# Attention and a mixture of experts on one core: the upper half of the hidden columns computed in transposed form

## The chip, the cores and the metric

The kernel runs on one core of a Trainium2 chip. The metric is device time in microseconds, the median of the timed runs. TensorE multiplies: the stationary operand is loaded as weights, the moving operand streams past it column by column, and results are summed in PSUM. ScalarE and VectorE work element by element, GpSimd issues the gathers and scatters, SyncE issues the other DMAs, in the order of its queue.

## The reference

Attention with a sigmoid in place of the softmax, then a mixture of eight experts, each token going to the one with the largest logit:

```python
B, heads, S, D = 8, 12, 448, 64          # 3584 tokens of width 768
attn = 1 / (1 + exp(-(q @ k.T / 8 - log(S))))
x = (attn @ v)                            # laid out as [3584, 768]
logits = normed(x) @ normed(expert_emb).T / tau
e = argmax(logits); gate_w = softmax(logits)[e]
for e in range(8):                        # w1 [768, 1024], w2 [1024, 768]
    h = maximum(x[mask] @ w1[e], 0)
    out[mask] = gate_w[mask] * (h @ w2[e])
```

## The kernel before

Attention comes first (to about 355 us of the span): 48 pairs of heads, scores, sigmoid and the product with v, with the routing worked out beside it. Then the expert stage. The tokens of an expert are cut into tiles of 128; a last piece of at most 64 tokens is a short tile. Two early tiles (numbers -2 and -1) of the expert with the most tokens are computed while the routing still runs, then tiles 0, 1, 2 and so on, 33 slots, of which 31 hold tokens here. Even slots take experts from the front and odd slots from the back, and each parity has its own buffers for w1 and w2, so that a new expert's weights are loaded for one parity while the other computes.

All values are split in two halves of 16 bits, hi and lo, and a product is three terms: hi x hi, hi x lo, lo x hi (`L1_TERMS`, `L2_TERMS`).

A tile t goes through these steps. GpSimd gathers its token rows (`xg`), SyncE transposes them by DMA to `xt`. Layer 1 has `xt` blocks stationary and w1 moving, 18 matmuls of 512 columns for each half of the 1024 hidden columns (`layer1_full`, L213); in a short tile the two halves run side by side in the two column halves of the array (`layer1_short`, L219). The result has tokens on partitions, in PSUM tile `pss`, one for each half. `hidden` then takes the ReLU, hi by ScalarE (L239), lo by VectorE (L240), to `hr`, and SyncE transposes `hr` by DMA to `hT` (L242), with hidden columns on partitions, as layer 2 needs it. Both halves do so, one after the other. Layer 2 has `hT` blocks stationary and w2 moving, 48 matmuls of 384 columns (L225, short: L232), lower half of the hidden columns first. The result is scaled and scattered to `out` (L780, L781, L912).

The order is written by hand. TensorE does layer 1 of tile t+1, then layer 2 of tile t. For the other engines a string, `ORD = "aGbLcdCDAMB"`, says the order of one step: small letters fetch weight blocks (a, d: halves of w2; b, c: halves of w1), capitals cast them, G gathers and transposes `xt` of tile t+3, L is layer 1 of t+1 with its ReLU and its transposes, M is layer 2 of t. SyncE's queue therefore holds, over one step and into the next: the transposes of `hT`, then c, d, a, then the transpose of `xt`, then b, and the next transposes of `hT`. Fetches and casts are skipped where the expert stays the same. Short or full is chosen at run time by a branch of TensorE (`tc.If(kind > 0)`), and both kinds are written out in its program.

Of the kernel before, what the change touches and what calls it, by code (L numbers as in the profile page):

```python
# [11 lines left out]
F16 = mybir.dt.float16  # L12
# [9 lines left out]
P = 128  # L22
# [11 lines left out]
NFC = F // P  # L34
# [15 lines left out]
ORD = "aGbLcdCDAMB"  # L50
ED = 2
# [58 lines left out]
def attn_moe_kernel(ctx: ExitStack, tc: tile.TileContext, q, k, v, emb, tau, w1, w2, consts, eye, out, dbg=None):  # L110
# [98 lines left out]
    L2_TERMS = [(fc, i, wi) for fc in range(NFC) for i, wi in ((0, 2), (0, 3), (1, 2))]  # L209

    def layer1_full(t, st, xt, half):
        for n, (kc, wi, xi) in enumerate(L1_TERMS):
            nc.tensor.matmul(ph[half][:, t % 2], xt[:, xi, kc, :], wts[st][wi][:, kc, half * HF:(half + 1) * HF],  # L213
                             start=(n == 0), stop=(n == len(L1_TERMS) - 1))

    def layer1_short(t, st, xt):
        for n, (kc, wi, xi) in enumerate(L1_TERMS):
            for s in range(2):
                nc.tensor.matmul(ph[0][s * HP:(s + 1) * HP, t % 2], xt[:, xi, kc, :HP], wts[st][wi][:, kc, s * HF:(s + 1) * HF],  # L219
                                 start=(n == 0), stop=(n == len(L1_TERMS) - 1))  # L220

# [6 lines left out]
    def layer2_short(st, hs, po):  # L228
        for n, (fc, i, wi) in enumerate(L2_TERMS):
            for d in range(2):  # L230
                s = fc // 4 * HP
                nc.tensor.matmul(po[0][d * HP:(d + 1) * HP, :HD], hs[0][:, i, fc % 4, s:s + HP],  # L232
                                 wts[st][wi][:, fc, d * HD:(d + 1) * HD],
                                 start=(n == 0), stop=(n == len(L2_TERMS) - 1))

    def hidden(t, half):
        ps = ph[half][:, t % 2]
        hr = bp2.tile([P, 2, HF], F16, name=f"hr{half}", bufs=1)
        mark[ET.Activation] = nc.scalar.activation(hr[:, 0], ps, AF.Relu)  # L239
        mark[ET.DVE] = nc.vector.scalar_tensor_tensor(hr[:, 1], ps, 0.0, hr[:, 0], op0=ALU.max, op1=ALU.subtract)  # L240
        h = bp2.tile([P, 2, HF // P, P], F16, name=f"hT{half}")
        mark[ET.SP] = nc.sync.dma_start_transpose(h.rearrange("f i c t -> f (i c) t"), hr.rearrange("t i f -> t (i f)"))  # L242
        hT[t, half] = h
# [12 lines left out]
    with ExitStack() as actx:  # L256
# [388 lines left out]
        layer1_full(-2, 0, xte[0], 0)  # L645
        hidden(-2, 0)
# [7 lines left out]
        layer1_full(-2, 0, xte[0], 1)  # L654
        hidden(-2, 1)
# [6 lines left out]
        layer1_full(-1, 0, xte[1], 0)  # L662
        psn = route2(NG - 1)
        hidden(-1, 0)
# [132 lines left out]
    layer1_full(-1, 0, xte[1], 1)  # L797
    hidden(-1, 1)
# [96 lines left out]
    def layer1(t, st, xt):  # L895
        kind = short(t)
        with pe_guard(t):
            with tc.If(kind > 0) as br:
                layer1_short(t, st, xt)
            with br.Else():  # L900
                for half in range(2):
                    layer1_full(t, st, xt, half)
        for half in range(2):
            hidden(t, half)
# [46 lines left out]
    for t in range(MAXL):  # L951
# [6 lines left out]
        if t == 0:  # L958
            layer1(1, 1, xg_t.pop(1))
            for n in range(2):  # L960
                reload(2, 0, n)
            place(wb[1][1:])
            for n in range(2):
                reload(1, 1, n)
            reload(3, 0, 1, fetch=True)
            reload(2, 1, 0, fetch=True)
            layer2(0, 0)
            reload(3, 0, 0)
            continue
        parts = {"a": (t + 1, 1, 1), "b": (t + 3, 0, 0), "c": (t + 3, 0, 1), "d": (t + 2, 1, 0)}  # L970
        casts = {"A": parts["a"], "B": parts["b"], "C": (t + 2, 0, 1), "D": (t + 1, 1, 0)}
# [38 lines left out]
```

## Time and profile before

| | |
|---|---|
| timed runs, median (lowest to highest of 3) | 887.71 us (884.38 to 889.79) |
| the profiled execution, whole time | 880.52 us |
| its span, first to last instruction | 878.7 us |
| mean granted clock of TensorE | 0.979 |
| TensorE busy | 825.4 us, 94% of the span |
| VectorE, ScalarE busy | 400.7 and 402.7 us, 46% each |
| DMA queue of SyncE | 63.9% of 16 engines' span |

Busy time of TensorE is the union of its matmuls; the mean length of one matmul is longer than the distance between two, since they are pipelined. Times in the rows below are counted from the start of the span. In a row of the timeline the first number is the start, the second the length of the stretch, xN the count of instructions, and in brackets the idle time just before it and what ended it. SPq stands for SyncE's queue.

### The profile page before, as it was taken

Reading aid. Unit: us, or ns where it says so; the run is one execution under the profiler, and the core shown is the slowest. Engines: PE = TensorE matmul, PEld = TensorE weight load, DVE = VectorE, ACT = ScalarE, POOL = GpSimd, SP = SyncE. Lnnn points to the kernel's source line nnn. Section 1 sums busy time; section 2 is a strip of 40 time slices with the busy share of each in tenths; the row PEclk is TensorE's granted clock in tenths of the full one; section 3 lists DMA queues with packets and bytes.
Section 4 is the critical chain, followed back from the end, with each engine's and each line's share of the span. In section 5 each row is a group of like instructions: output and inputs, shape, how many; then the busy total and the mean of one; then the engine's idle time right before and its main releaser. Section 6 shows DMA issues by size and latency. Waiting matters only on the chain. (4 is left out here: it accounts for less than half of the span.)

```text
span 878.7 us, 16153 instructions
## 1 busy us (share of the span) xinstructions
PE 825.4 (94%) x5384; PEld 402.3 (46%) x5384; DVE 400.7 (46%) x765; ACT 402.7 (46%) x616; POOL 180.4 (21%) x238
## 2 busy tenths in 40 slices
PE   6999999999999999998699999699999999999784
PEld 3444444444444443454345555355555555555342
DVE  4434354446576865776244116543510113515642
ACT  5667677767676766133133015433410113314541
POOL 2112121212121220123212212112222122223010
PEclk9999999999999999999989999899999999999897
DMA  5646475658797985969899579999996568879984
GB/s 148 165 112 195 122 194 148 174 136 201 209 243 198 266 200 170 199 144 240 196 274 183 127 191 301 252 223 246 261 163 136 104 134 234 236 195 273 283 210 85
DMA packets 260113, 170.67 MB, mean 194 GB/s; under 512 B 199804, under 2 KB 237158, under 8 KB 259984
## 3 DMA queue, kind: packets, MB, share of 16 engines
q1 hardware_dynamic: 249632, 132.96, 63.9%
q0 software_dynamic: 9360, 35.81, 13.1%
q8 instruction: 67, 1.10, 0.5%
q14 instruction: 62, 0.51, 0.2%
q10 hardware_dynamic: 992, 0.29, 0.1%
HBM read 103.80 MB, written 23.99 MB: 145 GB/s over the span
## 5 line engine op out<-in xcount | busy, mean ns | idle before, releaser
L213 PE MATMUL pss<-w,xt 128*128 128x512 f16 x900 | 198.5, 379 | 1.8 <-DVE hr L240 0.9
L225 PEld LDWEIGHTS <-hT 128*128 128x128 f16 x1296 | 129.2, 100 | 121.2 <-DMA hT<-hr 28.5
L355 ACT ACTIVATE att<-pss,bias_s 128x896 f32<-128x896 f32 x144 | 139.9, 1005 | 61.4 <-PE pss L353 57.8
L225 PE MATMUL psv<-w,hT 128*128 128x384 f16 x768 | 137.0, 341 | 26.7 <-DMA hT<-hr 26.2
L213 PEld LDWEIGHTS <-xt 128*128 128x128 f16 x900 | 87.4, 98 | 106.7 <-issue 3.6
L375 PE MATMUL psv<-att,vt 128*64 128x448 f32 x576 | 129.4, 556 | 0.0
L239 ACT ACTIVATE hr<-pss 128x512 f16<-128x512 f32 x70 | 39.3, 595 | 186.8 <-PE pss L213 135.1
L240 DVE SCALAR_TENSOR_TENSOR hr<-pss,hr 128x512 f16<-128x512 f32 x70 | 46.1, 688 | 157.6 <-ACT hr L239 133.4
L912 POOL DMA_INDIRECT out<-ob,six x64 | 70.6, 1103 | 190.7 <-ACTq L876 137.2
L353 PE MATMUL pss<-kq 64*128 64x448 f16 x864 | 99.4, 354 | 0.0
L312 POOL COPY pk<-qk 128x384 f32<-128x384 f32 x94 | 49.3, 525 | 189.7 <-PE ptr L322 115.2
L174 DVE SCALAR_TENSOR_TENSOR w<-stage_w,w 128x768 f16<-128x768 f32 (+1 forms) x78 | 76.0, 1004 | 25.5 <-ACT w L166 23.3
L225 PE MATMUL pso<-w,hT 128*128 128x384 f16 x528 | 87.6, 326 | 0.0
L166 ACT ACTIVATE w<-stage_w 128x768 f16<-128x768 f32 (+1 forms) x78 | 66.9, 878 | 37.9 <-DMA stage_w<-in_moe_w 30.5
L884 POOL DMA_INDIRECT xg<-xs,gix x33 | 34.4, 1043 | 191.0 <-DMA xt<-xg 155.0
L174 DVE SCALAR_TENSOR_TENSOR w<-stage,w 128x1024 f16<-128x1024 f32 (+1 forms) x48 | 55.2, 1174 | 19.0 <-ACT w L166 18.4
L353 PEld LDWEIGHTS <-kq 64*128 64x128 f16 x864 | 34.4, 94 | 63.7 <-issue 42.0
L342 DVE SCALAR_TENSOR_TENSOR kq<-ptr,kq 128x512 f16<-128x512 f32 x96 | 60.2, 649 | 3.5 <-ACT kq L339 3.2
L341 DVE TENSOR_SCALAR kq<-ptr 128x512 f16<-128x512 f32 x48 | 33.0, 688 | 62.1 <-PE ptr L322 62.0
L375 PEld LDWEIGHTS psv<-att,vt 128*64 128x64 f32 x576 | 32.8, 135 | 58.0 <-issue 57.2
L331 PE MATMUL ptr<-ident,pk 128*128 128x128 f32 x288 | 50.5, 286 | 7.3 <-DVE pk L312 4.7
L331 PEld LDWEIGHTS ptr<-ident,pk 128*128 128x128 f32 x288 | 33.6, 144 | 28.8 <-issue 18.1
(189 smaller groups left out, 628.5 us busy)
## 6 DMA issues: line engine op xcount, KB each, us to landing
stage_w<-in_moe_w SPq DMA_DIRECT2D x64, 384.0 KB
stage<-in_moe_w SPq DMA_DIRECT2D x40, 512.0 KB
qk<-in_q SPq DMA_DIRECT2D x48, 192.0 KB
qk<-in_k SPq DMA_DIRECT2D x48, 192.0 KB
vt<-in_v SPq DMA_DIRECT2D x48, 192.0 KB
xs<-xrow POOLq DMA_DIRECT2D x24, 384.0 KB
stage_w<-in_moe_w SPq DMA_DIRECT2D x14, 512.0 KB
stage<-in_moe_w SPq DMA_DIRECT2D x8, 384.0 KB
```

The lines of the kernel that those rows point to most:

```text
L166: nc.scalar.activation(wts[st][i][:, c, :], s, AF.Copy, scale=SW)
L174: nc.vector.scalar_tensor_tensor(wts[st][i + 1][:, c, :], s, SW, wts[st][i][:, c, :], op0=ALU.mult, op1=ALU.subtract)
L213: nc.tensor.matmul(ph[half][:, t % 2], xt[:, xi, kc, :], wts[st][wi][:, kc, half * HF:(half + 1) * HF], start=(n == 0), stop=(n == len(L1_ ...
L225: nc.tensor.matmul(po[d][:, :HD], hs[fc // 4][:, i, fc % 4, :], wts[st][wi][:, fc, d * HD:(d + 1) * HD], start=(n == 0), stop=(n == len(L2 ...
L240: mark[ET.DVE] = nc.vector.scalar_tensor_tensor(hr[:, 1], ps, 0.0, hr[:, 0], op0=ALU.max, op1=ALU.subtract)
L312: en.tensor_copy(t.rearrange("p c h d -> p h c d"), qk[i][:, j])
L331: nc.tensor.transpose(ps[:, o + c * P:o + (c + 1) * P], t[:, c].rearrange("p h d -> p (h d)"), ident)
L342: last_split[0] = nc.vector.scalar_tensor_tensor(lo, ps[:, :n], SQK, hi, op0=ALU.mult, op1=ALU.subtract)
L353: nc.tensor.matmul(ps[:, h, :S], x[r, ki, c * P:(c + 1) * P], x[r, qi, 512:], start=(n == 0), stop=(n == 2))
L355: sig[0] = nc.scalar.activation(a, ps[:, :, :S], AF.Sigmoid, bias=bias_s, scale=1.0 / (8.0 * SQK * SQK))
L375: nc.tensor.matmul(pav[i][h * D:(h + 1) * D, :S], w, m, start=(c == 0), stop=(c == CM))
L912: ins = mark[ET.Pool] = nc.gpsimd.indirect_dma_start(out.rearrange("n (h d) -> (n h) d", h=2), bass.IndirectOffsetOnAxis(ap=six[:, d, c:c ...
```

## The change

The lower half of the hidden columns stays as it is. For the upper half, blocks of w1 (128 columns each) become stationary and `xt` moves, 128 columns in a full tile and 64 in a short one. The result then has hidden columns on partitions, so that the ReLU writes it straight into `hT1`, and no DMA transpose follows. There are 72 matmuls for the upper half in place of 18. In a short tile the lower half alone is now split over the two column halves of the array, 256 columns each. The branch between short and full is taken once for the lower half and once for each two blocks of the upper half (`FB = 2`). Layer 2 takes the upper half first, and the fetches and casts of w2's halves are exchanged accordingly.

```diff
+FB = 2
...
-    L2_TERMS = [(fc, i, wi) for fc in range(NFC) for i, wi in ((0, 2), (0, 3), (1, 2))]
-
-    def layer1_full(t, st, xt, half):
+    L2_ORDER = [*range(NFC // 2, NFC), *range(NFC // 2)]
+    L2_TERMS = [(fc, i, wi) for fc in L2_ORDER for i, wi in ((0, 2), (0, 3), (1, 2))]
+
+    def layer1_rows(t, st, xt):
         for n, (kc, wi, xi) in enumerate(L1_TERMS):
-            nc.tensor.matmul(ph[half][:, t % 2], xt[:, xi, kc, :], wts[st][wi][:, kc, half * HF:(half + 1) * HF],
+            nc.tensor.matmul(ph[0][:, t % 2], xt[:, xi, kc, :], wts[st][wi][:, kc, :HF],
                              start=(n == 0), stop=(n == len(L1_TERMS) - 1))
 
-    def layer1_short(t, st, xt):
+    def layer1_rows_short(t, st, xt):
+        w = HF // 2
         for n, (kc, wi, xi) in enumerate(L1_TERMS):
             for s in range(2):
-                nc.tensor.matmul(ph[0][s * HP:(s + 1) * HP, t % 2], xt[:, xi, kc, :HP], wts[st][wi][:, kc, s * HF:(s + 1) * HF],
+                nc.tensor.matmul(ph[0][s * HP:(s + 1) * HP, t % 2, :w], xt[:, xi, kc, :HP], wts[st][wi][:, kc, s * w:(s + 1) * w],
                                  start=(n == 0), stop=(n == len(L1_TERMS) - 1))
+
+    def layer1_cols(t, st, xt, fs, n):
+        for f in fs:
+            for m, (kc, wi, xi) in enumerate(L1_TERMS):
+                nc.tensor.matmul(ph[1][:, t % 2, f % 4 * P:f % 4 * P + n], wts[st][wi][:, kc, f * P:(f + 1) * P], xt[:, xi, kc, :n],
+                                 start=(m == 0), stop=(m == len(L1_TERMS) - 1))
...
-    def hidden(t, half):
+    def relu(t, half, hi, lo):
         ps = ph[half][:, t % 2]
-        hr = bp2.tile([P, 2, HF], F16, name=f"hr{half}", bufs=1)
-        mark[ET.Activation] = nc.scalar.activation(hr[:, 0], ps, AF.Relu)
-        mark[ET.DVE] = nc.vector.scalar_tensor_tensor(hr[:, 1], ps, 0.0, hr[:, 0], op0=ALU.max, op1=ALU.subtract)
-        h = bp2.tile([P, 2, HF // P, P], F16, name=f"hT{half}")
+        mark[ET.Activation] = nc.scalar.activation(hi, ps, AF.Relu)
+        mark[ET.DVE] = nc.vector.scalar_tensor_tensor(lo, ps, 0.0, hi, op0=ALU.max, op1=ALU.subtract)
+
+    def hidden_rows(t):
+        hr = bp2.tile([P, 2, HF], F16, name="hr", bufs=1)
+        relu(t, 0, hr[:, 0], hr[:, 1])
+        h = bp2.tile([P, 2, HF // P, P], F16, name="hT0")
         mark[ET.SP] = nc.sync.dma_start_transpose(h.rearrange("f i c t -> f (i c) t"), hr.rearrange("t i f -> t (i f)"))
-        hT[t, half] = h
+        hT[t, 0] = h
+
+    def hidden_cols(t):
+        h = bp2.tile([P, 2, HF // P, P], F16, name="hT1")
+        relu(t, 1, *(h[:, i].rearrange("f c t -> f (c t)") for i in range(2)))
+        hT[t, 1] = h
...
             with tc.If(kind > 0) as br:
-                layer1_short(t, st, xt)
+                layer1_rows_short(t, st, xt)
             with br.Else():
-                for half in range(2):
-                    layer1_full(t, st, xt, half)
-        for half in range(2):
-            hidden(t, half)
+                layer1_rows(t, st, xt)
+        hidden_rows(t)
+        for f in range(4, NFC, FB):
+            with pe_guard(t):
+                with tc.If(kind > 0) as br:
+                    layer1_cols(t, st, xt, range(f, f + FB), HP)
+                with br.Else():
+                    layer1_cols(t, st, xt, range(f, f + FB), P)
+        hidden_cols(t)
...
-        parts = {"a": (t + 1, 1, 1), "b": (t + 3, 0, 0), "c": (t + 3, 0, 1), "d": (t + 2, 1, 0)}
-        casts = {"A": parts["a"], "B": parts["b"], "C": (t + 2, 0, 1), "D": (t + 1, 1, 0)}
+        parts = {"a": (t + 1, 1, 0), "b": (t + 3, 0, 0), "c": (t + 3, 0, 1), "d": (t + 2, 1, 1)}
+        casts = {"A": parts["a"], "B": parts["b"], "C": (t + 2, 0, 1), "D": (t + 1, 1, 1)}
```

In SyncE's queue, in a step of the expert stage, before: `hT` and `hr` of the two halves, then the fetches of c.

```order
L876 UNCONDITIONAL_BRANCH x8
L242 DMA_TRANSPOSE hT_6748<-hr_6745 128x8x128
L898 UNCONDITIONAL_BRANCH
L242 DMA_TRANSPOSE hT_6753<-hr_6750 128x8x128
L876 COMPARE_AND_BRANCH
L162 ISA
L162 DMA stage_w_6755<-in_moe_w 128x1024
```

The same place after:

```order
L892 UNCONDITIONAL_BRANCH x8
L914 UNCONDITIONAL_BRANCH
L253 DMA_TRANSPOSE hT_7464<-hr 128x8x128
L892 COMPARE_AND_BRANCH
L163 ISA
L163 DMA stage_w_7615<-in_moe_w 128x1024
```

One transpose is left, and the fetches of c follow it at once.

On TensorE, the end of layer 1 of a full tile and the start of layer 2 before; `w_0` and `w_2` are the hi parts of w1 and w2:

```order
L213 LDWEIGHTS xt
L213 MATMUL pss<-w_0_4272,xt 128x512
L898 UNCONDITIONAL_BRANCH
L876 UNCONDITIONAL_BRANCH x5
L791 COMPARE_AND_BRANCH
L232 LDWEIGHTS hT_7701
L232 MATMUL psv<-w_2_78,hT_7701 64x384
```

After, the end of the lower half of a full tile, where the upper half now follows (its first block for short tiles comes first in the program, the one for full tiles 72 rows behind it):

```order
L215 LDWEIGHTS xt
L215 MATMUL pss<-w_0_76,xt 128x512
L914 UNCONDITIONAL_BRANCH
L892 UNCONDITIONAL_BRANCH x3
L921 COMPARE_AND_BRANCH
L228 LDWEIGHTS w_0_76
L228 MATMUL pss<-xt,w_0_76 128x64
```

The stationary operand has changed from `xt` to w1, and between the halves of layer 1 there is now a branch, as there is one in the middle of the upper half. TensorE's program has 15,053 rows before and 23,827 after.

## Rows read from the trace of the kernel before

**Rows 1.** The page: the span, busy time of TensorE (PE) with its share and its count of instructions, and its busy tenths in 40 slices of the span.

```profile
span 878.7 us, 16153 instructions
PE 825.4 (94%) x5384; PEld 402.3 (46%) x5384; DVE 400.7 (46%) x765; ACT 402.7 (46%) x616; POOL 180.4 (21%) x238
...
PE   6999999999999999998699999699999999999784
```

**Rows 2.** Waits of TensorE by line and releaser: us in total, times, longest.

```profile
PE psv L225 <- DMA hT<-hr: 26.2, 5, 7.5
...
PE pso L232 <- DMA hT<-hr: 1.5, 2, 1.2
```

**Rows 3.** Timeline of TensorE's matmuls around the four longest waits for hT (L213 and L219 are layer 1 of full and short tiles, L225 and L232 layer 2).

```profile
426.01 7.93 PE L213 MATMUL pss<-w,xt 128*128 128x512 f16 x36 [0.16 <-SPq L876]
441.46 10.39 PE L225 MATMUL psv<-w,hT 128*128 128x384 f16 x48 [7.52 <-DMA hT<-hr]
451.69 7.93 PE L213 MATMUL pss<-w,xt 128*128 128x512 f16 x36
...
553.44 4.08 PE L219 MATMUL pss<-w,xt 128*64 128x512 f16 x36
564.24 10.44 PE L225 MATMUL psv<-w,hT 128*128 128x384 f16 x48 [6.72 <-DMA hT<-hr]
...
582.75 4.09 PE L232 MATMUL pso<-w,hT 128*64 128x384 f16 x48 [0.30 <-DMA hT<-hr]
...
805.67 7.94 PE L213 MATMUL pss<-w,xt 128*128 128x512 f16 x36
813.45 7.96 PE L225 MATMUL pso<-w,hT 128*128 128x384 f16 x48
821.34 4.08 PE L219 MATMUL pss<-w,xt 128*64 128x512 f16 x36
831.33 10.02 PE L225 MATMUL psv<-w,hT 128*128 128x384 f16 x48 [5.92 <-DMA hT<-hr]
841.19 7.93 PE L213 MATMUL pss<-w,xt 128*128 128x512 f16 x36
...
858.21 10.23 PE L225 MATMUL psv<-w,hT 128*128 128x384 f16 x48 [4.99 <-DMA hT<-hr]
```

**Rows 4.** Stretches of 3 us behind the first and the third of these waits: stretch, its length, busy time of TensorE and matmuls, granted clock, DMA share, GB/s.

```profile
441.46:444.46 3.00, 3.00 (x10) 0.50 1.01 307
...
831.33:834.33 3.00, 3.00 (x10) 0.50 0.99 291
```

**Rows 5.** Timeline of SyncE's queue: transposes of hidden blocks (L242) and fetches of w2 blocks (L162), start and time to issue.

```profile
433.05 7.14 SPq L242 DMA_TRANSPOSE hT<-hr  x2
...
492.15 2.64 SPq L242 DMA_TRANSPOSE hT<-hr  x2
...
544.19 10.47 SPq L162 DMA_DIRECT2D stage_w<-in_moe_w  x8
...
560.96 2.67 SPq L242 DMA_TRANSPOSE hT<-hr  x2
564.40 9.85 SPq L162 DMA_DIRECT2D stage_w<-in_moe_w  x8
...
579.48 2.64 SPq L242 DMA_TRANSPOSE hT<-hr  x2
...
828.05 2.64 SPq L242 DMA_TRANSPOSE hT<-hr  x2
...
845.21 2.65 SPq L242 DMA_TRANSPOSE hT<-hr  x2
```

**Rows 6.** Groups of TensorE's matmuls by line and shape: count, busy us, mean ns of one, idle time before.

```profile
L213 PE MATMUL pss<-w,xt 128*128 128x512 f16 x900 | 198.5, 379 | 1.8 <-DVE hr L240 0.9 <-issue 0.6 <-DVEq L876 0.2
...
L225 PE MATMUL pso<-w,hT 128*128 128x384 f16 x528 | 87.6, 326 | 0.0
...
L219 PE MATMUL pss<-w,xt 128*64 128x512 f16 x216 | 24.5, 380 | 0.2 <-issue 0.2
...
L397 PE MATMUL psl<-enT,xT 128*128 128x16 f16 x336 | 11.6, 170 | 0.9 <-DVE L L399 0.9
...
L757 PE MATMUL psr<-VG,POH 128*128 128x70 f16 x28 | 1.1, 196 | 0.6 <-DVE VG L753 0.6
```

**Rows 7.** Timeline of TensorE: two stretches of narrow matmuls, each matmul with a new 128x128 weight block (their groups are in rows 6).

```profile
361.14 0.75 PE L397 MATMUL psl<-enT,xT 128*128 128x16 f16 x24 [0.91 <-DVE L L399]
...
397.03 1.11 PE L757 MATMUL psr<-VG,POH 128*128 128x70 f16 x28 [0.60 <-DVE VG L753]
```

**Rows 8.** Three stretches of 4 us in which no weights are fetched; columns: busy time (and instructions) of TensorE, weight loads, VectorE, ScalarE and GpSimd, granted clock, DMA share, GB/s.

```profile
486.00:490.00 4.00, 4.00 (x21) 1.81 (x19) 0.00 (x0) 0.00 (x0) 1.20 (x2) 1.00 0.28 82
490.00:494.00 4.00, 4.00 (x25) 2.30 (x24) 1.29 (x2) 1.09 (x2) 0.00 (x0) 1.00 0.37 102
494.00:498.00 4.00, 4.00 (x27) 2.44 (x25) 0.00 (x0) 0.00 (x0) 0.00 (x0) 1.00 0.94 106
```

**Rows 9.** Timeline: VectorE's cast (lo part) of the last w1 block of the next expert before the layer 1 at 451.69.

```profile
448.78 1.23 DVE L174 SCALAR_TENSOR_TENSOR w<-stage,w 128x1024 f16<-128x1024 f32 x1 [0.38 <-ACTq L876]
```

**Rows 10.** The chain that ended last: start, length, what; the transpose ahead of the layer 2 at 582.75.

```profile
579.48 3.19 DMA hT<-hr
```

**Rows 11.** DMA queues: the larger of the two instruction queues with packets, MB and share of 16 engines' span.

```profile
q8 instruction: 67, 1.10, 0.5%
```

More of the change, by code (lines that the diff above doesn't have):

```diff
@@ L229, in layer2_short @@
         for n, (fc, i, wi) in enumerate(L2_TERMS):
+            x = hs[1][:, i, fc % 4, :HP] if fc >= 4 else hs[0][:, i, fc % 2, fc // 2 * HP:(fc // 2 + 1) * HP]
             for d in range(2):
-                s = fc // 4 * HP
-                nc.tensor.matmul(po[0][d * HP:(d + 1) * HP, :HD], hs[0][:, i, fc % 4, s:s + HP],
-                                 wts[st][wi][:, fc, d * HD:(d + 1) * HD],
+                nc.tensor.matmul(po[0][d * HP:(d + 1) * HP, :HD], x, wts[st][wi][:, fc, d * HD:(d + 1) * HD],
                                  start=(n == 0), stop=(n == len(L2_TERMS) - 1))
-    def hidden(t, half):
+    def relu(t, half, hi, lo):
         ps = ph[half][:, t % 2]
-        hr = bp2.tile([P, 2, HF], F16, name=f"hr{half}", bufs=1)
-        mark[ET.Activation] = nc.scalar.activation(hr[:, 0], ps, AF.Relu)
-        mark[ET.DVE] = nc.vector.scalar_tensor_tensor(hr[:, 1], ps, 0.0, hr[:, 0], op0=ALU.max, op1=ALU.subtract)
-        h = bp2.tile([P, 2, HF // P, P], F16, name=f"hT{half}")
-        mark[ET.SP] = nc.sync.dma_start_transpose(h.rearrange("f i c t -> f (i c) t"), hr.rearrange("t i f -> t (i f)"))
-        hT[t, half] = h
+        mark[ET.Activation] = nc.scalar.activation(hi, ps, AF.Relu)
[4 more added lines that the diff above has]
+        h = bp2.tile([P, 2, HF // P, P], F16, name="hT0")
+        mark[ET.SP] = nc.sync.dma_start_transpose(h.rearrange("f i c t -> f (i c) t"), hr.rearrange("t i f -> t (i f)"))
+        hT[t, 0] = h
[3 more added lines that the diff above has]
+        hT[t, 1] = h
     def pe_guard(t):
@@ L644, in attn_moe_kernel @@
         ph[0] = ps_s.tile([P, 2, 512], F32, name="pss")
-        layer1_full(-2, 0, xte[0], 0)
-        hidden(-2, 0)
+        layer1_rows(-2, 0, xte[0])
+        hidden_rows(-2)
         for c in (2, CM):
@@ L653, in attn_moe_kernel @@
         place(wp.pop(0)[1][1:])
-        layer1_full(-2, 0, xte[0], 1)
-        hidden(-2, 1)
+        layer1_cols(-2, 0, xte[0], range(4, NFC), P)
+        hidden_cols(-2)
         with tc.high_priority():
@@ L661, in attn_moe_kernel @@
                 rows(*rowq.pop(0))
-        layer1_full(-1, 0, xte[1], 0)
+        layer1_rows(-1, 0, xte[1])
         psn = route2(NG - 1)
-        hidden(-1, 0)
+        hidden_rows(-1)
     bp1 = ctx2.enter_context(tc.tile_pool(name="bp1", bufs=1, side="right", reuse_waits="tile"))
@@ L795, in layer2 @@
         evac2(t, pd, bp3.tile([P, DM], F32, name="ob", bufs=2))
-    layer1_full(-1, 0, xte[1], 1)
-    hidden(-1, 1)
+    layer1_cols(-1, 0, xte[1], range(4, NFC), P)
+    hidden_cols(-1)
     po[0][1] = ps_v.tile([P, 512], F32, name="psv")
@@ L965, in attn_moe_kernel @@
             reload(3, 0, 1, fetch=True)
-            reload(2, 1, 0, fetch=True)
+            reload(2, 1, 1, fetch=True)
             layer2(0, 0)
```

## The prediction

> **What bounds the kernel now.** I read the page first: TensorE is busy for 825.4 of 878.7 us, and the slices show it full nearly everywhere in the second half, which is the expert stage, with dents near its start, past its middle and at the end [rows 1]. The waits of TensorE say what the dents are: by far the longest line is for hT, the hidden block after its DMA transpose, 26.2 us in five waits ahead of full tiles, and another 1.5 us ahead of short ones [rows 2]. The timeline of TensorE shows where: 7.52, 6.72, 5.92 and 4.99 us before layer 2 of four tiles, together 25.2 us [rows 3]. A dent costs more than its gap: the layer 2 behind it takes 10.39, 10.44, 10.02 and 10.23 us where an undisturbed one takes 7.96, another 9.2 us, because after the idle time the granted clock is 0.50 (1.2 of 2.4 GHz) for the first 3 us, shown for the first and the third [rows 3, 4]. So some 34 us of the span hang on transposes that come late; elsewhere TensorE runs without a gap, and there each nanosecond added to a matmul is a nanosecond of the span.
>
> Why the transposes are late is in the queue of SyncE: the transposes of a tile stand behind the weight blocks of the next expert. At 544.19 eight blocks take 10.47 us, the pair of transposes comes at 560.96, and TensorE starts at 564.24, 3.3 us after that issue [rows 3, 5]. At 579.48, 828.05 and 845.21 it is the same pattern, behind what was queued first [rows 5]. At 433.05 the pair takes 7.14 us to be issued [rows 5].
>
> **The change, part by part.** *Layer 1, full tile.* The lower half stays as it is: 18 matmuls of 512 columns. The upper half goes from 18 of 512 to 72 of 128, each with a weight load of its own. In a run of 36 the start to start of a 512-column matmul is (7.93 - 0.379) / 35 = 215.7 ns; for 384 columns it is (7.96 - 0.33) / 47 = 162.4 ns [rows 3, 6]. The difference over 128 columns is 0.416 ns a column, and 2.5 ns a matmul remain. No row has a 128-column f16 matmul with its own weights. The nearest narrow one has 70 columns and a new 128x128 weight block each time: 28 take 1.11 us, (1.11 - 0.20) / 27 = 33.8 ns, which is 29.2 for the columns and 4.6 over [rows 6, 7]. So 128 columns take 53.3 + 2.5 = 55.8 to 53.3 + 4.6 = 57.9 ns; I take the middle, 56.8, and 72 of them take 4.09 us against 18 x 215.7 = 3.88. That is +0.21 us (0.13 to 0.29) a tile. 25 full tiles come from the 900 matmuls [rows 6], two more are the early tiles: 27 x 0.21 = **+5.7 us** (3.5 to 7.8).
>
> *Layer 1, short tile.* The 36 matmuls of 512 columns run two at a time in column halves, 4.08 us [rows 3]. They become 36 of 256, about half of that, 2.0 us, and 72 of 64 columns at 31 to 33.8 ns, 2.2 to 2.4 us. That is +0.2 to +0.4 us, six tiles (216 matmuls) [rows 6], **+1.8 us**.
>
> *ReLU and layer 2.* ScalarE and VectorE do the same two operations a half, on as many elements; only the place of the upper half's result differs. Cost nothing. Layer 2 has the same matmuls in another order, and w2's halves swap places in the fetch order with it. Cost nothing, since the swap keeps the half that is needed first in the step that was first.
>
> *Transposes.* SyncE issues one a tile, not two. A transpose costs SyncE some 1.3 us where nothing presses (2.64 for two) [rows 5], and it costs the DMA engines: with a pair issued at 492.15, the shares 0.37 and 0.94 of two windows of 4 us hold 5.2 us, of which about 2.2 would be there without the pair (0.28 in the window ahead), so 1.5 us for one, an estimate [rows 5, 8]. Where weights fill the DMA engines, each transpose left out lets what follows in SyncE's queue come 1.3 to 2.8 us sooner.
>
> *The wait itself.* Layer 2 now begins with the half that needs no DMA, and reaches the other one 3.9 us later (2.0 in a short tile). I follow the three places with the landing times as they are and then move them.
>
> First dent: layer 1 ends at 433.94, the upper half is through at 437.85, the lower block lands at 441.46, and layer 2 ends at 445.4, not 451.69, a gain of 6.3. But the next layer 1 has a new w1, whose last block is cast until 448.78 + 1.23 = 450.0 [rows 9]; it is the sixth of six blocks, wanted 3.2 us into the layer, so the layer can't begin without loss before 446.8: 4.9 us. With two transposes fewer ahead the blocks come 2 to 4 us sooner. I take **6.5** (4.9 to 9).
>
> Second dent: layer 1 ends at 557.52, the upper half at 561.4; landing unmoved at 564.24 leaves a wait of 2.8, less than half of 6.72; I count no clock loss for it. But the next tile's transposes come at 579.48 and land 3.19 us later [rows 10], so TensorE would get there early and wait again: layer 2 to 568.1, layer 1 to 575.9, short upper half to 577.9, wait to 582.7, end 584.7 against 586.84, only 2.1 us. The queue there is weight traffic from 544 on; two or three transposes fewer move the second landing by 3 to 6 us. I take **5.5** (2.1 to 8).
>
> Third dent, to the end: layer 1 ends at 825.42, upper half 829.3, landing 831.33, layer 2 to 835.2, layer 1 to 843.0, short upper half to 845.0, its lower block at 845.21 + 3.3 = 848.5, end 850.5, upper half of the last tile 854.4, lower block 858.0, end 862.1 against 868.44, 6.3 us. With three pairs cut to one each, the last landing comes 4 to 8 us sooner; without any wait the end would be at 825.4 + 7.9 + 7.8 + 4.0 + 7.8 = 852.9. I take **9.5** (6.3 to 14).
>
> *Sum.* 6.5 + 5.5 + 9.5 = 21.5 us gained (13.3 to 31), 7.5 paid, net 14. The profiled execution took 880.52 us: 866.5. The median of the timed runs, 887.71, is 7.2 above that execution; carried over, **873.7**, which I round to 873.
>
> **Rivals.** *(a) The queue gives all of it back.* The DMA engines are freer than I allow and all dents close, 31 us: 880.5 - 31 + 7.5 + 7.2 = 864. For it speaks that DMA shares are near 1 in the dents [rows 4]; against it the new w1 at 450.0 [rows 9].
>
> *(b) The weights are the bound.* The landings don't move, since the blocks of weights set the queue's pace: 13.3 gained, 7.5 paid, 880.5 - 13.3 + 7.5 + 7.2 = 882. The eight blocks at 544.19 and 564.40 speak for it, 1.2 to 1.3 us each in issue alone [rows 5].
>
> *(c) Slower: narrow matmuls don't hide their weight loads.* In the upper half every matmul has its own load. The fastest stream of such pairs, 16 columns wide, runs at (0.75 - 0.17) / 23 = 25.2 ns a pair [rows 6, 7]. If such a load stood beside the columns rather than under them, a pair would take 53.3 + 25.2 = 78.5 ns, 72 of them 5.65 us, +1.77 a tile, 48 us in all: 880.5 - 21.5 + 48 + 1.8 + 7.2 = 916. The change loses from 3.88 us + 21.5/27 on, which is 65 ns a pair. The 70-column pairs at 33.8, not 54, speak against it; but there are only 28 of them in a row, so a queue filled ahead may have carried them. The Trainium skill (TensorE: Matmul & The Clock Gate, section Back-to-back issue gap) speaks for it: in streams of load and matmul it gives some 81 ns a matmul of 128 columns, and 56 only for the isolated gap; by 81 the upper half would take 5.83 us and the sum would be 921, an estimate. The same section gives 131 ns for 512 columns where the row here shows 215.7, so I trust it little.
>
> *(d) Slower: the instructions don't come in time.* TensorE's program grows from 15,053 to 23,827 rows, as both kinds of tile are written out for two column steps, 266 rows more a tile, most of them jumped over. The instruction queue with the larger blocks brought 67 packets in 0.5% of 16 engines' span, 1.05 us each [rows 11]. If one more such packet a tile were waited for, 33 tiles: +35, 909. Against it: before, the jumps over 72 and 96 rows of the short kind ahead of 805.67 and 813.45 leave no gap [rows 3]. The Trainium skill (Runtime: NRT & Kernel Launch, section Instruction fetch mechanics) says that a taken branch to a target outside the pages at hand stalls for a fetch; the jumps here are at most some 100 rows.
>
> **How the numbers follow.** Forecast 0.45, (a) 0.14, (b) 0.25, (c) 0.08, (d) 0.08. About 1% (8.9 us) is what a measurement of this kernel can tell from no change. Forecast and (a) lie beyond it, (b) within, (c) and (d) on the slow side: 0.59, 0.25, 0.16. The range runs from 860, under (a), to 897, past (b) and the mild end of (c); what is left out is most of (c) and (d) and little below.
>
> **What would show it.** In the profile after: 72 matmuls of 128 columns in about 4.1 us, start to start 56 to 58 ns; the waits of TensorE for hT under 10 us in all; layer 2 behind the former dents at 7.9 us and the clock at 1.0; hT issued 35 times, not 70. If the waits for hT are still above 12 us, (b) holds; if layer 1 of a full tile takes over 8.6 us with a gap inside, (d); without a gap, (c). I would also be wrong if TensorE's wait moves to w1 or w2 blocks in the place of hT.

## The result and the profile after

The changed kernel took 893.14 us (median of 20 runs, 884.69 to 898.59), the kernel before 888.03 on the same chips (20 runs, 877.33 to 895.64): a ratio of 1.0073 with a 95% interval of 1.0045 to 1.0101. It is slower by some 6.5 us, where I had forecast 14 us faster. The profiled execution took 893.61 us with a span of 891.9 us; that of before had a span of 878.7 and was itself 7.5 us under its median, so the two traces differ by 13.2 us, where the medians differ by 5.1.

The page after (compare [rows 1, 11]): span, busy times, TensorE's tenths, and the instruction queue with packets, MB and share.

```profile
span 891.9 us, 19953 instructions
...
PE 837.7 (94%) x7274; PEld 478.5 (54%) x7274; DVE 399.0 (45%) x765; ACT 402.1 (45%) x616; POOL 181.2 (20%) x238
...
PE   6999999999999999998799979899899999989974
...
q8 instruction: 101, 1.65, 0.8%
```

TensorE is busy 12.3 us longer, and of the slices of the expert stage, which before had dents down to 0.6, eight now stand at 0.7 or 0.8 ahead of the last. The instruction queue brought 101 packets where it brought 67 [rows 11]. TensorE's program grew by 8,774 rows, which is 258 rows for each of the 34 packets.

Waits of TensorE after (in us, times, longest), where [rows 2] stood before; L234 is layer 2 of a full tile, L228 the new upper half.

```profile
PE pso L234 <- issue: 7.6, 3, 4.9
PE psv L234 <- ACT w L167: 5.6, 2, 3.0
PE psv L234 <- PEq L920: 5.1, 1, 5.1
...
PE pss L228 <- issue: 3.3, 2, 2.4
PE psv L234 <- DMA hT<-hr: 3.1, 1, 3.1
PE pso L241 <- DMA hT<-hr: 1.6, 1, 1.6
```

The waits for hT fell from 27.7 to 4.7 us, as the forecast said. In their place stand waits that mostly name no data: "issue" (nothing that the profile shows), and PEq, TensorE's own sequencer. The two of `psv` that are put down to a cast of w stand at places of the same kind as the others, and with `FB = 4`, below, the first of them names "issue" (565.54). The timeline of TensorE's matmuls says where they are.

```profile
397.14 2.16 PE L222 MATMUL pss<-w,xt 128*64 128x256 f16 x36 [0.19 <-DVEq L892]
399.23 1.90 PE L228 MATMUL pss<-xt,w 128*128 128x64 f16 x59
403.49 0.54 PE L228 MATMUL pss<-xt,w 128*128 128x64 f16 x13 [2.37 <-issue]
...
442.58 6.99 PE L234 MATMUL psv<-w,hT 128*128 128x384 f16 x24 [3.15 <-DMA hT<-hr]
...
568.42 9.44 PE L234 MATMUL psv<-w,hT 128*128 128x384 f16 x48 [2.56 <-ACT w L167]
...
629.03 9.65 PE L234 MATMUL psv<-w,hT 128*128 128x384 f16 x48 [3.01 <-ACT w L167]
...
800.39 9.50 PE L234 MATMUL pso<-w,hT 128*128 128x384 f16 x48 [2.43 <-issue]
...
870.07 10.49 PE L234 MATMUL psv<-w,hT 128*128 128x384 f16 x48 [5.13 <-PEq L920]
```

Every short tile (L222) has a gap behind or inside its upper half, and the last gap, 5.13 us, lies where the whole layer 1 of an empty slot is jumped over. Two smaller ones lie at full tiles, 1.41 us inside the layer 2 at 552.01 and 1.35 us ahead of that at 738.49. The largest one behind a short tile shows best that no data is awaited. All engines around it:

```profile
514.41 2.27 PE L228 MATMUL pss<-xt,w 128*128 128x64 f16 x72
...
516.72 0.60 ACT L246 ACTIVATE hT<-pss 128x512 f16<-128x512 f32 x1 [1.60 <-PE pss L228]
517.35 0.69 DVE L247 SCALAR_TENSOR_TENSOR hT<-pss,hT 128x512 f16<-128x512 f32 x1 [1.51 <-ACTq L892]
518.23 1.01 SPq L163 DMA_DIRECT2D stage_w<-in_moe_w  x2
519.56 0.96 SPq L163 DMA_DIRECT2D stage<-in_moe_w  x1
521.59 0.13 PEld L234 LDWEIGHTS <-hT 128*128 128x128 f16 x2 [5.03 <-issue]
521.59 1.78 PE L234 MATMUL pso<-w,hT 128*128 128x384 f16 x5 [4.91 <-issue]
```

TensorE's matmuls end at 516.68. ScalarE and VectorE finish with the short tile at 518.04 and have nothing further for it, the next layer 2 belongs to the full tile before it, and TensorE still stands until 521.59.

What it waits for can be seen in the DMA queue of the instructions. Of the stretches 516.68 to 519.1, 519.1 to 520.2 and 520.2 to 521.59 us, only the middle one has a packet of that queue start in it:

```profile
q8 instruction: 1, 0.02, 6.0%
```

By the trace's record of this packet it runs from 519.13 to 520.18, and TensorE goes on 1.41 us after its end. It is the same at the others: before the restarts at 403.49, 521.59, 555.54, 568.42, 629.03, 738.49, 800.39 and 844.24 the last packet of q8 ended 1.3 to 1.8 us earlier, and 2.0 us at the empty slot. Before the restarts after the four long waits for hT in the trace of before, it ended 13.3, 5.3, 5.5 and 2.7 us earlier. A distance so even, with 77 packets in the 497 us behind 395, points to instructions that TensorE waited for, also where the profile names a cast of w.

As behind the old dents [rows 4], the clock is low after the gap: its stretch, length, busy time of TensorE, weight loads, VectorE, ScalarE, GpSimd, then granted clock, DMA share, GB/s.

```profile
521.59:524.59 3.00, 3.00 (x10) 1.49 (x11) 0.00 (x0) 0.00 (x0) 0.00 (x0) 0.50 0.69 80
568.42:571.42 3.00, 3.00 (x10) 1.48 (x11) 0.09 (x2) 0.84 (x1) 0.00 (x0) 0.50 0.93 338
```

**Where the 13.2 us come from.** All waits of TensorE from 385 us of the span on, as the timeline gives them, sum to 32.0 us, against 30.2: +1.8. Layer 2 behind a gap takes 9.63, 10.64, 9.44, 9.65, 9.50 and 10.49 us instead of 7.96, 11.6 us over, and 3.0 more behind the hT wait at 442.58 (24 matmuls in 6.99 instead of 4.0): 14.6 us of slow clock, against 9.2 before: +5.4. The narrow matmuls cost 5.5 (worked out below). Together +12.7. Seen the other way: the waits for hT and the slow clock behind them fell from 36.9 us (27.7 and 9.2) to 7.7 (4.7 and 3.0), 29.2 gained; other waits rose from 2.5 to 27.3 us, with 11.6 of slow clock behind them, 36.4 lost. With the narrow matmuls this gives the +12.7.

### The profile page after: what moved, and what is told of

Read it like the earlier page. It is cut to its first block, busy times and chain, and to the rows that moved or that the text cites. A ratio compares the mean times of both kernels' runs of the same rounds, so it can differ in the third digit from the quotient of the medians.

```text
span 891.9 us, 19953 instructions
## 1 busy us (share of the span) xinstructions
PE 837.7 (94%) x7274; PEld 478.5 (54%) x7274; DVE 399.0 (45%) x765; ACT 402.1 (45%) x616; POOL 181.2 (20%) x238
## 5 line engine op out<-in xcount | busy, mean ns | idle before, releaser
L234 PEld LDWEIGHTS <-hT 128*128 128x128 f16 x1296 | 129.9, 102 | 117.9 <-issue 40.1
L371 ACT ACTIVATE att<-pss,bias_s 128x896 f32<-128x896 f32 x144 | 139.8, 1005 | 61.5 <-PE pss L369 57.9
L234 PE MATMUL psv<-w,hT 128*128 128x384 f16 x768 | 138.4, 343 | 15.1 <-ACT w L167 5.6
L228 PEld LDWEIGHTS <-w 128*128 128x128 f16 x2376 | 123.9, 98 | 11.3 <-issue 5.4
L228 PE MATMUL pss<-xt,w 128*128 128x128 f16 (+1 forms) x2232 | 118.7, 214 | 3.3 <-issue 3.3
L215 PE MATMUL pss<-w,xt 128*128 128x512 f16 x450 | 101.2, 379 | 1.6 <-DVE w L175 1.0
L234 PE MATMUL pso<-w,hT 128*128 128x384 f16 x528 | 92.0, 336 | 10.4 <-issue 7.6
L175 DVE SCALAR_TENSOR_TENSOR w<-stage_w,w 128x768 f16<-128x768 f32 (+1 forms) x78 | 74.1, 1000 | 21.6 <-ACT w L167 18.7
L215 PEld LDWEIGHTS <-xt 128*128 128x128 f16 x450 | 43.5, 98 | 53.1 <-issue 2.9
L900 POOL DMA_INDIRECT xg<-xs,gix x33 | 36.8, 1114 | 145.9 <-DMA xt<-xg 85.3
L246 ACT ACTIVATE hT<-pss 128x512 f16<-128x512 f32 x35 | 20.9, 596 | 88.5 <-PE pss L228 82.2
L246 ACT ACTIVATE hr<-pss 128x512 f16<-128x512 f32 x35 | 20.9, 596 | 86.8 <-PE pss L215 53.6
```

Source lines behind the costliest of these rows:

```text
L175: nc.vector.scalar_tensor_tensor(wts[st][i + 1][:, c, :], s, SW, wts[st][i][:, c, :], op0=ALU.mult, op1=ALU.subtract)
L215: nc.tensor.matmul(ph[0][:, t % 2], xt[:, xi, kc, :], wts[st][wi][:, kc, :HF], start=(n == 0), stop=(n == len(L1_TERMS) - 1))
L228: nc.tensor.matmul(ph[1][:, t % 2, f % 4 * P:f % 4 * P + n], wts[st][wi][:, kc, f * P:(f + 1) * P], xt[:, xi, kc, :n], start=(m == 0), sto ...
L234: nc.tensor.matmul(po[d][:, :HD], hs[fc // 4][:, i, fc % 4, :], wts[st][wi][:, fc, d * HD:(d + 1) * HD], start=(n == 0), stop=(n == len(L2 ...
L246: mark[ET.Activation] = nc.scalar.activation(hi, ps, AF.Relu)
L371: sig[0] = nc.scalar.activation(a, ps[:, :, :S], AF.Sigmoid, bias=bias_s, scale=1.0 / (8.0 * SQK * SQK))
```

## The experiments

Ten kernels ran. The theory that they test (theory 1 in the expectations): TensorE's program has become too long for what brings its instructions, and shows it where many rows are passed in little time. Its rivals: the number of branches, the 64-column pairs themselves, and the traffic of the weights.

**One width for the upper half.** The upper half takes 128 columns in short tiles too, so no second copy of it is written out and no branch stands in it (18,885 rows for TensorE).

```diff
-        for f in range(4, NFC, FB):
-            with pe_guard(t):
-                with tc.If(kind > 0) as br:
-                    layer1_cols(t, st, xt, range(f, f + FB), HP)
-                with br.Else():
-                    layer1_cols(t, st, xt, range(f, f + FB), P)
+        with pe_guard(t):
+            layer1_cols(t, st, xt, range(4, NFC), P)
```

> The changed kernel, but the upper half is always computed 128 columns wide, in short tiles too, so that it needs no branch: TensorE's program shrinks from 23,827 to 18,885 rows, and a short tile pays 72 x (55.8 - 31) ns = 1.8 us more in layer 1, six times, 10.7 us. Theory 1, the instructions come too late (the sequencer passes some 500 rows, most of them jumped over, in the 4.3 us of a short tile, and then waits for its program): the gaps behind short tiles, 2.4 to 4.9 us each with 1.5 to 2.7 us of slow clock behind them, some 24 us in all, close for the most part, and the time falls by 8 to 14 us against the changed kernel, to about 880. Theory 2, layer 2 waits there for something of the data path (the ReLU that now writes hT1, or weights): the gaps stay, and the time rises by 11 to about 904. Theory 3, the pairs of 64 columns at 31 ns outrun the sequencer's decoding, whatever the length of the program: the gaps close as in theory 1.

Measured: 871.05 us against 883.93 for the kernel before on that chip, ratio 0.9841 (0.9788 to 0.9895), although each short tile computes 64 columns for nothing, some 2 us. Its longest waits by the timeline of TensorE:

```profile
447.03 6.02 PE L234 MATMUL psv<-w,hT 128*128 128x384 f16 x24 [7.39 <-DMA hT<-hr]
...
855.35 1.80 PE L234 MATMUL psv<-w,hT 128*128 128x384 f16 x10 [2.56 <-issue]
```

The gaps behind layer 1 of the six short tiles are gone (0.77 us in a layer 2 of one is the longest left at them); one wait for hT and the jump over an empty slot are left. That refutes theory 2, by which the gaps would have stayed. The run takes away the 64-column pairs, the branches and the length at once, so it doesn't say which of them it was.

**Fewer branches.** `FB = 4` puts the upper half into one branch instead of two; the length stays (23,713 rows).

> The changed kernel with FB = 4: one branch for the four upper blocks and not two, the same matmuls, nearly the same rows (23,713). Theory 1 (length of program): within 5 us of the changed kernel, since the same rows are passed. A fourth theory, that each branch costs TensorE time of its own at the decision: a third of the branches in layer 1 goes, the gaps behind short tiles shrink by a third or more, and the time falls by 8 us or more, to 885 or below.

Measured: 891.54 us, ratio to before 1.0097 (1.0061 to 1.0132), as the changed kernel. The gap at the same place is that of the changed kernel:

```profile
520.88 10.37 PE L234 MATMUL pso<-w,hT 128*128 128x384 f16 x48 [4.82 <-issue]
...
565.54 9.66 PE L234 MATMUL psv<-w,hT 128*128 128x384 f16 x48 [2.26 <-issue]
```

Some full tiles now have gaps of 0.2 to 1.1 us inside their upper half. With a third of the branches of layer 1 gone the time did not fall, so their number is not the cause.

**Dead rows, first attempt.** The kernel before with two questions behind each layer 1 that are never answered with yes, over 72 and 61 matmuls; these never run.

```diff
...
+        for m in (72, 61):
+            with pe_guard(t):
+                with tc.If(kind > 1):
+                    for n in range(m):
+                        nc.tensor.matmul(ph[1][:, t % 2, :P], wts[st][0][:, 0, :P], xt[:, 0, 0, :],
+                                         start=(n == 0), stop=(n == m - 1))
```

> The kernel before with nothing added but rows that are never executed: behind layer 1 of each tile two branches that are never taken into 72 and 61 matmuls with their loads, 266 rows a tile, so that TensorE's program has 23,994 rows, as many as the changed kernel's 23,827. All matmuls, transposes and waits that run are those of before. Theory 1 (instructions come too late): gaps of 2 to 5 us appear behind the short tiles with the slow clock after them, and the time rises by 10 to 25 us, to 898 to 913. Theories 2 and 3 (data path, decoding of narrow pairs): no change beyond the two branches a tile, under 3 us, 888 to 891.

Measured: 921.4 us, ratio 1.0424 (1.0362 to 1.0485). The theory had the sign, but neither the size (10 to 25 us more; it was 37.5) nor the place:

```profile
483.06 7.97 PE L225 MATMUL psv<-w,hT 128*128 128x384 f16 x48 [0.99 <-ACT hr L239]
...
516.74 7.97 PE L225 MATMUL psv<-w,hT 128*128 128x384 f16 x48 [1.11 <-PEq L905]
```

Full tiles too have a gap of about 1.1 us, half a microsecond for each question added. No instruction packet ends in the 3 us before the restarts at 483.06 and 516.74, so these are not gaps of the kind seen above. That cost is not in the changed kernel, nearly all of whose full tiles run without a gap, so this run can't tell length from questions. A test without that cost follows below.

**Short tiles as before, full tiles as changed.** Lower and upper half of a short tile run side by side with 512 columns, as in the kernel before, and layer 2 of a short tile takes both from the transposed block (18,936 rows).

```diff
...
         hidden_rows(t)
-        for f in range(4, NFC, FB):
-            with pe_guard(t):
-                with tc.If(kind > 0) as br:
-                    layer1_cols(t, st, xt, range(f, f + FB), HP)
-                with br.Else():
-                    layer1_cols(t, st, xt, range(f, f + FB), P)
+        with pe_guard(t):
+            with tc.If(kind < 1):
+                layer1_cols(t, st, xt, range(4, NFC), P)
```

> Full tiles as in the changed kernel, short tiles as before (both halves in rows of 512 columns side by side, one transpose, layer 2 from that alone); the upper half is one block under one branch that short tiles skip. 18,936 rows. Theory 1: a short tile passes fewer rows and its layer 1 lasts 4.0 us at a slow pace of instructions, so most of the gaps behind short tiles close: about 20 us below the changed kernel, some 873, and below before. Theory 2: gaps stay, within 4 us of the changed kernel. Theory 3: gaps close, as there are no 64-column pairs any more.

Measured: 869.41 us, the lowest of the kernels that do the whole work (the 871.05 of one width is too near to tell apart), ratio to before 0.9825 (0.9773 to 0.9877): 14.5 us gained, where the forecast for the changed kernel was 14. Theory 1 had expected some 873. The run doesn't separate theory 1 from theory 3, since the 64-column pairs are gone too. What waits are left, by the timeline:

```profile
517.96 9.65 PE L233 MATMUL pso<-w,hT 128*128 128x384 f16 x48 [2.74 <-ACTq L891]
...
618.08 7.97 PE L233 MATMUL psv<-w,hT 128*128 128x384 f16 x48 [0.47 <-PEq L919]
...
844.29 4.09 PE L240 MATMUL pso<-w,hT 128*64 128x384 f16 x48 [2.90 <-DMA hT<-hr]
851.41 9.65 PE L233 MATMUL psv<-w,hT 128*128 128x384 f16 x48 [3.02 <-issue]
```

**Dead rows, balanced.** Now the dead matmuls stand in the Else of a second question inside the short kind's branch, in layer 1 and in layer 2, so that a full tile takes no question more and only jumps further. Every matmul that runs is that of the kernel before.

```diff
...
-                layer1_short(t, st, xt)
+                with tc.If(kind < 2) as br2:
+                    layer1_short(t, st, xt)
+                with br2.Else():
+                    for n in range(66):
+                        nc.tensor.matmul(ph[0][:, t % 2], xt[:, 0, 0, :], wts[st][0][:, 0, :HF], start=(n == 0), stop=(n == 65))
```

> The kernel before, with 66 matmuls that never run in layer 1 and 66 in layer 2 of every tile, both in the Else of a second question that stands inside the short kind's branch: a full tile jumps over them with the jump that it takes anyway, a short tile answers one question more. TensorE's program grows from 15,053 to 23,897 rows, as many as the changed kernel has; every matmul that runs, every transfer and every wait is that of the kernel before, and no tile has a matmul of 64 or 128 columns. Theory 1 (the program is too long for its supply: rows that are jumped over have to come too, and TensorE outruns them where a short tile passes many rows in little time): the gaps of 2 to 5 us behind the short tiles appear here too, with nothing of the change in it, and the kernel is 8 to 25 us slower than before. Theory 2 (the rows are not the cause: the pairs of 64 columns, some 30 ns each, outrun TensorE's sequencer): no new gap, within 3 us of before. The instruction queue's packets go from 67 to about 100 under both.

Measured: 911.34 us against 884.82, ratio 1.0322 (1.0268 to 1.0376), 101 instruction packets. The edit shown is that of layer 1; layer 2 has the like. The profiled execution, 902.12 us, is the shortest of five. The timeline of TensorE (L213 and L219 are layer 1 of full and short tiles, L225 and L232 layer 2):

```profile
616.39 7.96 PE L225 MATMUL pso<-w,hT 128*128 128x384 f16 x48
624.29 4.08 PE L219 MATMUL pss<-w,xt 128*64 128x512 f16 x36
630.90 7.97 PE L225 MATMUL psv<-w,hT 128*128 128x384 f16 x48 [2.54 <-ACT w L166]
638.71 7.93 PE L213 MATMUL pss<-w,xt 128*128 128x512 f16 x36
646.58 4.09 PE L232 MATMUL pso<-w,hT 128*64 128x384 f16 x48
653.64 10.88 PE L213 MATMUL pss<-w,xt 128*128 128x512 f16 x36 [2.98 <-issue]
```

No tile here has a narrow matmul, and the gaps are of the kind that the changed kernel has: 2.54 us behind layer 1 of the short tile, 2.98 behind its layer 2, none behind the full tiles of this stretch. From 390 us on, TensorE's waits that name neither hT nor SyncE's queue sum to 27.7 us (without 1.0 us of the routing), nearly all around the six short tiles; the one behind a full layer 1 is 1.90 us at 554.00. Of the eleven over 1 us, ten begin to run again 1.4 to 1.8 us after the end of an instruction packet, as in the changed kernel. The rival with the 64-column pairs falls: it expected no new gap.

**The control, and half the length.** The same with 2 and with 33 dead matmuls in each place.

> The kernel with dead rows in balanced questions, with 2 dead matmuls in place of 66 in each place: the question that a short tile answers twice more is there, the length is not (15,450 rows for TensorE against 15,053 before and 23,897 with 66). It is the control for the run with 66, which was 3.2% slower than before. Theory 1 (the length does it): within 5 us of before, gaps behind short tiles at most 1 us each. Rival (the question itself stalls TensorE, whatever is jumped over): 15 to 28 us slower than before, as with 66.

> The same with 33 dead matmuls in each place, half as many (19,541 rows). If each row that is jumped over costs the same, half of what 66 cost over 2: some +11 to +15 us over before. If there is a length that is covered and only what is beyond it costs (the kernels of 18,885 and 18,936 rows with narrow matmuls in full tiles were faster than before), under +8 us. If the question does it and not the length: +15 to +28 us.

Measured: with 2 (15,450 rows), 885.58 us against 884.98, ratio 1.0018 (0.9978 to 1.0057), no new gap behind short tiles. With 33 (19,541 rows), 895.75, ratio 1.0103 (1.0058 to 1.0147). With 66, above, 1.0322. So the questions cost nothing beyond 0.6%, and the length costs 0, 1 and 3%; with 33, 10.8 us by the medians, just short of the 11 to 15 that an equal price for each row would give, with an interval of 5 to 13 us that reaches into the other expectation, under 8. But with 33 only one gap is of the kind seen with 66; the rest of its loss in the trace is in longer waits for transposes, 39.0 us in all against 29.7 with 2, and that execution, 901.95 us, was 6.2 us above the median. Two of its rows:

```profile
574.85 10.88 PE L225 MATMUL psv<-w,hT 128*128 128x384 f16 x48 [9.63 <-DMA hT<-hr]
...
637.35 7.97 PE L225 MATMUL psv<-w,hT 128*128 128x384 f16 x48 [3.31 <-ACT w L166]
```

The second is the gap of the kind seen with 66: an instruction packet ended 1.55 us before it. Why the transposes came later with 33 dead matmuls I could not settle.

**Without the traffic of the weights.** In the changed kernel and in that before, no expert's weights are fetched or cast after the first set (`ci[:, 0]`, the flag for a new expert, is zero).

```diff
-        nc.vector.tensor_tensor(ci[:, 0], ch, vd, op=ALU.mult)
+        nc.vector.tensor_scalar(ci[:, 0], ch, 0.0, None, op0=ALU.mult)
```

> The changed kernel in which no expert's weights are fetched or cast again after the first set, so that all tiles are computed with the weights that are there: left out are the later experts' weights. TensorE's program, jumps and matmuls are those of the changed kernel, the DMA queues of the expert stage are nearly empty. Theory 1a (the instructions come late because the blocks of weights fill the DMA engines that bring them): the gaps behind short tiles shrink below 1 us each, and the span is 5 to 10 us over that of the kernel before without reloads. Theory 1b (so many rows take their time even with idle DMA engines): gaps of 2 to 5 us behind short tiles stay, and the span is 15 to 30 us over that of the kernel before without reloads.

> The kernel before with the same part left out: no expert's weights are fetched or cast again. It is the mate of the run on the changed kernel without reloads. Both theories: no wait for hT above 1 us in the expert stage, since nothing is queued ahead of the transposes; 840 to 860 us. The difference of the two spans is then what the change's matmuls and its program cost, without the waits that it removes: +5 to +10 us by theory 1a, +15 to +30 us by theory 1b.

Measured: 872.58 us changed, 848.96 before, spans 869.1 and 845.6: a difference of 23.5 us. The changed one, around one short tile and at the empty slot:

```profile
609.30 2.15 PE L222 MATMUL pss<-w,xt 128*64 128x256 f16 x36
611.39 1.24 PE L228 MATMUL pss<-xt,w 128*128 128x64 f16 x31
613.02 0.31 PE L228 MATMUL pss<-xt,w 128*128 128x64 f16 x5 [0.39 <-issue]
613.77 0.28 PE L228 MATMUL pss<-xt,w 128*128 128x64 f16 x4 [0.43 <-issue]
614.48 1.10 PE L228 MATMUL pss<-xt,w 128*128 128x64 f16 x32 [0.43 <-issue]
615.55 7.97 PE L234 MATMUL psv<-w,hT 128*128 128x384 f16 x48
...
849.10 9.65 PE L234 MATMUL psv<-w,hT 128*128 128x384 f16 x48 [4.57 <-PEq L920]
```

And that before at the same tile, without any gap, and at the empty slot:

```profile
600.27 4.08 PE L219 MATMUL pss<-w,xt 128*64 128x512 f16 x36
604.28 7.97 PE L225 MATMUL psv<-w,hT 128*128 128x384 f16 x48
...
828.37 7.97 PE L225 MATMUL psv<-w,hT 128*128 128x384 f16 x48 [1.01 <-DMA hT<-hr]
```

By the total, the theory that instructions are late even with idle DMA engines holds (it said 15 to 30), though 5.5 of the 23.5 us are the narrow matmuls. By the gaps, both have a part: each is under 1.5 us at the short tiles instead of 2.4 to 4.9, and split up, so that from the start of layer 1 of the short tile to layer 2 it takes 6.25 us where the matmuls alone take 4.4; the jump over the empty slot stays at 4.57 us. So loaded DMA engines lengthen the gaps at short tiles; they don't make them. Full tiles without a gap follow each other in these two runs at 15.70 us (upper halves at 446.11 and 461.81) and 15.57 us (layers 1 at 459.14 and 474.71): the narrow matmuls cost a full tile 0.13 us.

**The order alone.** The kernel with short tiles as before, with layer 2 put back to lower half first, and w2's halves fetched in the order of before.

```diff
-    L2_ORDER = [*range(NFC // 2, NFC), *range(NFC // 2)]
+    L2_ORDER = [*range(NFC)]
```

> The kernel with full tiles as changed and short tiles as before (869.4), and layer 2 put back to the order of before, lower half first, with the w2 halves fetched in the order of before; the number of rows is unchanged at 18,936. It prices the order alone. Theory of the forecast (layer 2 waited for the transposes, and starting with the half that needs none is what gained): the waits for hT ahead of full tiles come back, 10 to 25 us in all with the slow clock behind them, and the time goes to 880 to 892. Rival (one transpose a tile instead of two is what gained, since SyncE's queue is shorter): waits for hT stay under 8 us in all, and the time is within 4 us of 869.4.

Measured: 876.05 us, ratio to before 0.9902 (0.9863 to 0.9941), between the two expectations: 8.8 us under before, where the kernel with the order was 14.5 under before in its own set of runs, 5.7 us between them. Its waits of TensorE:

```profile
PE psv L233 <- DMA hT<-hr: 10.4, 3, 6.0
...
PE pso L240 <- DMA hT<-hr: 1.2, 1, 1.2
```

Waits for hT are 11.6 us, against 4.5 with the order and 27.7 before. This execution, 882.39 us, was the longest of ten, so the usual one waits less. So the gain has two parts: the order is worth some 6 us, and the larger one stays without it. That part holds two things that no run separates: one transpose a tile instead of two, and its time. The one transpose is issued 2.6 us before the end of layer 1 (at 734.50, end 737.14, in the changed kernel), the pair of before 1.4 us after it (at 492.15, end 490.76).

## Why the prediction failed, step by step

**The four dents** (21.5 us of gain, 13.3 to 31): right in mechanism, and rather low. In the changed kernel waits for hT fell by 23 us and the slow clock behind them by 6.2, where part of it may come from the new gaps, which give the transposes time; the kernel with short tiles as before gained 14.5 us, which with 3.8 us paid for its full tiles is some 18 gross, though it keeps a few gaps for instructions itself.

**Narrow matmuls in full tiles** (56.8 ns, bounds 55.8 to 57.9; +5.7 us): right in kind and a little high. One row of the trace after, of a tile with a full upper half:

```profile
535.96 4.18 PE L228 MATMUL pss<-xt,w 128*128 128x128 f16 x72
```

(4.18 - 0.219) / 71 = 55.8 ns, the lower bound, with 219 ns the mean of one. 72 of them take 0.14 us more than 18 x 215.7 ns, for 27 tiles 3.8 us. Rival (c) is refuted: from 65 ns on the change would have lost. The 81 ns that the Trainium skill gives for a stream of such pairs (TensorE: Matmul & The Clock Gate, section Back-to-back issue gap) isn't what this stream runs at; the trace decides.

**Short tiles** (+1.8 us): the matmuls as worked out, 516.68 - 512.32 = 4.36 us instead of 4.08, six times 0.28, 1.7 us.

**Rival (d), instructions that don't come in time**: this is the step that failed. The sum put the longer program at nothing, and I had (d) at 0.08 and 909 us, with +35 us, a packet's 1.05 us in each of 33 tiles. The runs showed 21.7 us of gaps behind short tiles and at the empty slot (2.37 + 4.91 + 2.56 + 3.01 + 2.43 + 0.91 + 0.40 + 5.13), 2.8 more at two full tiles (1.41 + 1.35) and 11.6 of slow clock behind them, 36.1 together. That this is near +35 is luck: it comes from ten gaps, not from 33 tiles, from waits of up to 5 us, not of one packet's transfer, and a third of it is clock. The place was not as I looked for it either: layer 1 of a full tile still takes 4.05 + 4.18 us without a gap.

What led me wrong is the sentence set against it: that jumps over 72 and 96 rows leave no gap in the trace before [rows 3]. That is true of a program of 15,053 rows, and does not carry over to a longer one. The run with 66 dead matmuls does the same work as the kernel before with jumps over 132 rows more, and has the gaps; with 2 it has none. It is not the length of a jump alone, since full tiles jump over the same dead rows there. A full tile, with some 8 us of matmuls in either layer, shows few gaps in either kernel (1.41 and 1.35 us in the changed one, 1.90 with 66 dead matmuls); a short one passes as many rows of program with 4 us in either layer, and has them; an empty slot has no work at all. By the Trainium skill (Runtime: NRT & Kernel Launch, section Instruction fetch mechanics) a taken branch to a target outside the pages at hand waits for a fetch. These runs agree, with restarts 1.3 to 1.8 us after the end of an instruction packet. I had read the rule and argued it away with the length of one jump, where the rows to be passed for each tile, set against its work, were what mattered.

**The sum.** Not the terms in it but one left out of it. The range, 860 to 897, contains 893.14 by luck: it reached there for (b) and the mild end of (c), neither of which came about. The likeliest case, 873, was 20 us off and on the wrong side of no change. Of the signs listed for the profile after, three came as said or nearly (waits for hT under 10 us; 55.8 ns, just under the 56 to 58 named; hT issued 35 times). The clock and the 7.9 us of layer 2 behind the former dents did not come at the first one, which waits 3.15 us in the middle of its layer 2 and then runs slow (granted clock 0.50 from 442.58 on). The sign named for (d), a full layer 1 over 8.6 us, did not come, and (d) held nevertheless.

**What is open.** Of the 4.91 us at 516.68, 2.45 pass until the packet starts, 1.05 in its transfer and 1.41 until TensorE goes on. What starts a packet so late was not measured, nor whether the length of the whole program matters beside the rows passed at each tile, nor why 33 dead matmuls go with longer waits for transposes.

## What to carry to other kernels

Code that is jumped over is not free: count the rows of program that an engine passes for each tile against the time its work gives it, take the tile with the least work (short, or empty), and don't conclude from a jump without a gap in a shorter program that a longer one has none. Where a kernel has a common and a rare case, write the costly new form for the common case alone: here that turned a loss of 0.7% into a gain of 1.7%. When one wait goes, look first at what hides behind the same idle time: the slow clock behind the gaps cost about another half of their length here (11.6 us on 24.5).

## What the runs showed of the hardware

- A pair of weight load and matmul with 128 columns runs at 55.8 ns in a stream of 72, one with 64 columns at (2.27 - 0.193) / 71 = 29 ns (0.193 us is the mean of one). At the 0.416 ns a column worked out from the kernel before, 64 columns are 26.6 ns, so the load adds 2.6 ns at most.
- A question ahead of a block that isn't run costs TensorE about 0.5 us where the block has no Else (1.1 us for two in each full tile; 0.47 us behind several short tiles in the fastest kernel), while two questions with an Else on the way of a short tile leave no gap there (ratio 1.0018, 0.9978 to 1.0057). Whether it is the question or the jump over so many rows was not separated.
- With idle DMA engines, the changed kernel runs the 72 narrow matmuls of a short tile in portions of 31, 5, 4 and 32, with 0.4 us between them.
- TensorE stands 4.6 us with idle DMA engines and 5.1 with busy ones at the layer 1 of an empty slot in the kernel with 23,827 rows, 3.0 in that with 18,936, and 1.0, put down to hT, in that with 15,053 rows and idle DMA engines.
- TensorE ran dry and went on 1.3 to 1.8 us after the end of an instruction packet at eight places of the changed kernel and at ten of that with 66 dead matmuls, whatever the profile named as the releaser (issue, a cast of w, a ReLU, a sequencer).
